# Moving the last two pa products of batch 1 ahead of the steps, and the activations' last subtractions of steps 1 to 11 to GpSimd

## The chip, the cores and the metric

The kernel runs on one core of a Trainium2 chip. The metric is the device time of one execution in microseconds, as the median of several runs; the core has five engines with queues of their own: TensorE (PE in the profile, with its weight loads as PEld), VectorE (DVE), ScalarE (ACT), GpSimd (POOL) and SyncE (SP), which here only issues transfers. ScalarE and GpSimd issue some transfers too. Each engine works through its own instructions in order and waits at an instruction until what it needs is there.

## The reference

A filter along the sequence by real Fourier transforms, and then an activation block on every token:

```
x: (8, 3008, 256)   filt_r, filt_i: (1505, 256)
w_in: (256, 2048)   w_out: (2048, 256)

X = rfft(x, axis=1)
Y = X * (filt_r + 1j * filt_i)
y = irfft(Y, n=3008, axis=1)

h = y.reshape(24064, 256) @ w_in
g = h / (1 + exp(-h))
out = g @ w_out
```

All is float32, and the weights arrive in a wider type (64-bit floats) that the kernel turns into float32 itself.

## The kernel before

**The activation block.** The tokens of a batch are taken in two halves of three pairs each, so there are 48 pairs (`token_pairs`), each of 2 x 256 tokens (240 in the last pair of a half). A pair takes eight steps, one for each pair of 128-wide slices of the 2048 hidden channels, so there are 384 steps. Both products are done as 2 x 2 blocks with seven products instead of eight. `hidden(step)` does the first seven (into the PSUM tiles `px` and `pyz`), with the sums between them: DVE forms g0, g2 and g1 from a product in PSUM and a copy in `abc` that ScalarE made, ScalarE applies silu to them, and DVE subtracts g[4:6] = g[1:3] - g[0:2]. `finish` makes the last two combinations, g6 = g2 - g4 and g7 = g3 - g6, and is called in the next step, right behind that step's g0. `project(step)` does the seven products of the second block into four accumulators `acc`; it runs one step later (`LAG = 1`), its products alternating with those of `hidden`. In it g6 and g7 are read by the last two products. `tokens(pair)` makes `ty`, the three combinations of y that the first products of a pair need.

**The order.** Nothing is scheduled automatically. Each step is cut into eight rounds. Every other piece of work (the Fourier stages of the next batches, the conversion of the weights, stores) is put at a step and a round by `put(step, rnd, piece)`; the list is sorted, and `until` emits the pieces whose time has come between the products of a step. So the place of a piece decides where it stands in each engine's queue. The first two pairs of batch 0 are taken in four parts (`PARTS`): steps 0 and 1 are of pair 0, steps 2 to 5 of pair 1, steps 6 to 11 of pair 0, and 12 to 15 of pair 1.

**The Fourier stages.** The sequence of 3008 is split as 94 rows by 32 columns. `pa` products (stage 1) transform the rows, `pb` products with the table `d_t` the columns, the filter is applied by DVE, `pc` products with `e_t` go back over the columns, and `pd` products (stage 3) with `wi_t` over the rows, giving y. Between the stages data go through DRAM (`d1`, `d2`) to change their layout. Batch 0 does all of this ahead of step 0, in room that later holds weights (`w_t`), with products that fill PE's pauses (`idle`); the other batches do it beside the steps of the batch before.

**Stage 1 of batch 1.** Eight units of x. Units 0 to 5 are three pairs p = 0, 1, 2, done ahead of step 0: `load_pair(p)` brings x in three 32-row slices for four column groups at once, `stage1_pair(p)` does 12 products on slices of 32 rows (line 432) into four PSUM banks, `out_pair` copies the banks out, and `store_rows` stores a unit with four transfers from GpSimd's queue. Units 6 and 7 are done in steps 7 and 8: `load_x` brings each to `x_all`, `stage1` does two products on 96 rows (line 452), ScalarE copies them out, and `store_rows` stores them. Their results are first read when batch 1's pb products begin, in step 11.

**PSUM banks ahead of step 0** are handed out in turn from eight (`bank`, counted by `early[0]`); a product waits until the bank's last content is copied out.

**The weights.** Sixteen tiles j, two for each pair of slices. A tile is loaded as raw words (`weights`), and converted in four parts on DVE with two activations on ScalarE between them: `bits` (lines 1222 and 1224), `converted` (ScalarE, lines 1231 and 1232), `added` (line 1238), `signed` (line 1243) and `placed` (line 1250), which writes w_t. When both tiles of a pair jp are placed, `combine_weights(jp)` makes the three combined blocks by four additions and subtractions. Tiles 0 to 3 are done ahead of step 0 and tiles 4 to 15 in steps 0 to 11, each before the step that reads it; the combining of jp 1 to 6 is done by GpSimd, of jp 0 and 7 by DVE.

**The order around the change**, ahead of step 0: the products of the pairs 0, 1 and 2, four idle products, then

```
    part["stage3"](0)
    part["stage3"](1)
    placed(2)
    part["stage3"](2)
    part["stage3"](3)
    placed(3)
    combine_weights(1, eng=gp)
    for u in range(4, 6):
        second["store_rows"](u)
    for g in (2, 3, 4, 5, 0, 1):
        for i in range(2):
            part["store_half"](g, i, 1, gp)
```

Here `stage3(g)` is 64 small pd products and the copying of their two banks to y, on ScalarE and DVE. `store_half(..., 1, ...)` stores the second half of the pc results, which stage 3 reads from step 11 on. `fetch_rows` (line 747) brings the first half back in the layout that the pd products of g = 0 to 3 read; the last fetch is issued by SP and ScalarE together.

Of the kernel before, what the change touches and what calls it, by code (L numbers as in the profile page):

```python
# [56 lines left out]
NS, NG = 24, 6  # L57
# [65 lines left out]
def second_pairs(x):  # L123

    rows = np.zeros((96, 32, C), x.dtype)
    rows[0:NR] = x.reshape(NR, 32, C)
    return rows.reshape(3, 32, 4, 4, 2 * C).transpose(2, 3, 1, 0, 4)[0:3].reshape(3, 128, 6 * C)
# [145 lines left out]
def kernel(  # L273
# [96 lines left out]
    def spectral(b):  # L370
# [54 lines left out]
        def stage1_pair(p):  # L425
# [406 lines left out]
        return dict(us=us, store_half=store_half, load_pair=load_pair, stage1_pair=stage1_pair, out_pair=out_pair, store_rows=store_rows, evict_y=evict_y, halves=halves, load_first=load_first, stage1_first=stage1_first, load_x=load_x, stage1=stage1, reverse_x=reverse_x,  # L832
# [15 lines left out]
    def plan(b, part):  # L848
# [153 lines left out]
    def tokens(pair):  # L1002

        n, yt = pairs[pair][3], channels(pair)
        t = typool.tile([128, 4, CH], FP32, name=f"ty_{pair}", tag="ty")
        combine(v, t[:, 0:2, 0:n], yt[:, :, n:2 * n],
                yt[:, 0, 0:2 * n].rearrange("p (a n) -> p a n", a=2), ALU.subtract)
        combine(v, t[:, 2, 0:n], yt[:, 1, n:2 * n], t[:, 0, 0:n], ALU.subtract)
        combine(v, t[:, 3, 0:n], yt[:, 1, 0:n], t[:, 2, 0:n], ALU.subtract)
        ty[pair] = t  # L1010

    def hidden(step):
# [24 lines left out]
        finish()  # L1037
# [295 lines left out]
    v.memset(blank, 0.0)  # L1333
    idle(12, operand=blank)
# [50 lines left out]
    part["forward"](5)  # L1385
    products(4)
# [57 lines left out]
    weights(4, 5)  # L1444
    second["load_x"](6)
    weights(6)
    second["load_x"](7)
# [9 lines left out]
    for step, rnd, *todo in (  # L1457
            (0, 5, (bits, 4)), (1, 0, (weights, 7, 8), (converted, 4)), (1, 1, (added, 4), (bits, 5), (signed, 4)),
            (1, 2, (weights, 9, 10)), (1, 5, (placed, 4), (added, 5)), (2, 0, (converted, 5)),
            (2, 1, (bits, 6), (signed, 5), (placed, 5)), (2, 3, (combine_weights, 2, None, gp)), (2, 5, (added, 6)),  # L1460
            (3, 0, (converted, 6)), (3, 1, (bits, 7), (signed, 6), (placed, 6)), (3, 3, (weights, 11)),
            (3, 5, (converted, 7), (added, 7)), (4, 1, (signed, 7), (placed, 7), (bits, 8)),
            (4, 3, (combine_weights, 3, None, gp), (weights, 12)), (4, 5, (converted, 8), (added, 8)),
            (5, 1, (signed, 8), (placed, 8), (bits, 9)), (5, 3, (weights, 13)), (5, 5, (converted, 9), (added, 9)),
            (6, 1, (signed, 9), (placed, 9), (bits, 10)), (6, 3, (combine_weights, 4, None, gp), (weights, 14)),
            (6, 5, (converted, 10)), (7, 1, (rounded, 10), (placed, 10)), (7, 2, (weights, 15)),
            (7, 3, (bits, 11), (added, 11)), (7, 5, (converted, 11), (bits, 12)), (8, 0, (converted, 12)),
            (8, 1, (signed, 11), (placed, 11), (added, 12)), (8, 2, (combine_weights, 5, None, gp)),
            (8, 3, (signed, 12), (placed, 12)), (8, 5, (bits, 13), (added, 13)), (9, 0, (converted, 13)),
            (9, 1, (bits, 14), (signed, 13), (placed, 13)), (9, 2, (combine_weights, 6, None, gp)),  # L1470
            (9, 5, (converted, 14), (added, 14), (bits, 15)), (10, 0, (converted, 15)),
            (10, 1, (signed, 14), (placed, 14), (added, 15)), (10, 5, (signed, 15), (placed, 15), (combine_weights, 7, 0)),
            (11, 1, (combine_weights, 7, 1))):
# [24 lines left out]
    for step in range(n_steps + LAG):  # L1498
# [3 lines left out]
        else:  # L1502
            finish()
# [51 lines left out]
```

## Time and profile before

| | us |
| --- | --- |
| median of 3 runs | 2499.95 (2499.06 to 2500.76) |
| the profiled execution | 2500.93 |
| its span, first to last instruction | 2499.1 |
| PE busy | 2479.1 |
| DVE busy | 1761.5 |
| ScalarE busy | 1092.3 |
| GpSimd busy | 458.4 |
| first pd product | 50.3 |
| first px product (start of step 0) | 56.7 |
| first px product of step 1 | 64.2 |
| first px product of step 11 | 135.8 |

The page gives each engine's busy time and, in 40 slices, how much of each slice it was busy. The chain that ended last is followed back from the last instruction, at each step to what released it. Groups of instructions are named by line, engine and operation, with what is written and read, and the idle time ahead of them with what ended it. The name in front of an arrow "<-" after an idle time is the engine and line that was waited for; "issue" is time in which the engine waited for nothing that the profile shows. Views of a stretch of time (timeline, busy times by stretch) use microseconds from the span's start. Outside the first 150 us and the last 100, PE is busy nearly without pause: 1600 us of the 1600 from 400 to 2000 us.

### The profile page before, as it was taken

To read this page: it belongs to the slowest core of one execution; us is meant where nothing else is said; L and a number is where in the kernel's file an instruction comes from. 1 tells how busy PE (TensorE), PEld (TensorE's weight loads), DVE (VectorE), ACT (ScalarE), POOL (GpSimd) and SP (SyncE) were. 2 spreads that over 40 slices of the span, in tenths; PEclk is the share of its full clock that TensorE was granted. 3 is DMA by queue.
4 is the path that set the end of the run, shared out by engine and by line. 5 is a ranking of instruction groups with operands and counts; after the bars stand their busy time and mean duration, and the time that the engine had idled before them with its cause. 6 is when DMAs were issued, how large, how long until landed. Compare 5 with 4: busy or idle time off the path is not lost.

```text
span 2499.1 us, 42322 instructions
## 1 busy us (share of the span) xinstructions
PE 2479.1 (99%) x16234; PEld 2125.2 (85%) x16234; DVE 1761.5 (70%) x3593; ACT 1092.3 (44%) x3001; POOL 458.4 (18%) x708
## 2 busy tenths in 40 slices
PE   9999999999999999999999999999999999999999
PEld 6778888888888888888888888889888888888988
DVE  7876677777777777777777867777677767655544
ACT  3634444444444444444444444444444444444443
POOL 4421112112121122211122112211221111101100
PEclk9999999999999999999999999999999999999999
DMA  8433233213242032420333203321142211200000
GB/s 303 147 88 103 67 72 82 72 37 81 60 96 72 23 93 53 114 63 20 82 75 100 55 26 91 79 68 43 35 107 54 56 43 35 63 21 9 17 9 17
DMA packets 139771, 170.68 MB, mean 68 GB/s; under 512 B 21053, under 2 KB 113565, under 8 KB 139037
## 3 DMA queue, kind: packets, MB, share of 16 engines
q1 hardware_dynamic: 115952, 121.15, 18.4%
q0 software_dynamic: 22656, 45.68, 7.0%
q8 instruction: 127, 2.08, 0.3%
q10 hardware_dynamic: 960, 1.16, 0.1%
q14 instruction: 76, 0.61, 0.1%
HBM read 96.06 MB, written 81.26 MB: 71 GB/s over the span
## 4 chain that ended last, share of the span: by engine, by line
PE 96%; DVE 2%; ACT 0%; issue 0%; POOL 0%; DMA 0%; DVEq 0%; POOLq 0%
PE acc L1093 45%; PE px L1025 25%; PE pyz L1025 19%; PE pd L800 1%; PE pf L522 1%; PE pc L618 1%; PE pb L580 1%; DVE g L996 1%; PE pc L696 0%; PE pa L402 0%; PE pb L562 0%; PE pd L762 0%; PE pa L432 0%; PE idle L1322 0%; DVE w_t L1250 0%
## 5 line engine op out<-in xcount | busy, mean ns | idle before, releaser
L1093 PE MATMUL acc<-g,w_t 128*128 128x256 f32 (+1 forms) x5376 | 1508.6, 376 | 3.2 <-ACT o L813 2.5
L1093 PEld LDWEIGHTS acc<-g,w_t 128*128 128x128 f32 x5376 | 1017.1, 190 | 153.5 <-ACT o L813 15.3
L996 DVE TENSOR_TENSOR g<-pyz,abc 128x256 f32<-128x256 f32 (+1 forms) x1152 | 479.6, 416 | 471.3 <-ACT abc L1046 231.4
L996 DVE TENSOR_TENSOR g<-g 128x256 f32<-128x256 f32 (+3 forms) x1152 | 591.2, 513 | 197.1 <-ACT g L1029 184.0
L1025 PE MATMUL px<-ty,w_t 128*128 128x256 f32 (+1 forms) x2304 | 677.5, 376 | 1.0 <-DVE ty L996 0.5
L1029 ACT ACTIVATE g<-g 128x256 f32<-128x256 f32 (+1 forms) x1152 | 472.8, 411 | 242.5 <-DVE g L996 242.5
L996 POOL TENSOR_TENSOR s<-s 128x256 f32<-128x256 f32 (+1 forms) x329 | 252.3, 784 | 1403.6 <-DVE s L1118 1044.8
L1025 PEld LDWEIGHTS px<-ty,w_t 128*128 128x128 f32 x2304 | 435.5, 190 | 55.9 <-issue 1.8
L1025 PE MATMUL pyz<-y,w_t 128*128 128x256 f32 (+1 forms) x1536 | 453.0, 377 | 6.6 <-DVE g L996 6.4
L1025 PEld LDWEIGHTS pyz<-y,w_t 128*128 128x128 f32 x1536 | 283.0, 190 | 52.9 <-DVE g L996 12.1
L1040 ACT COPY abc<-px 128x256 f32<-128x256 f32 (+1 forms) x384 | 141.3, 368 | 371.2 <-PE px L1025 371.2
L1046 ACT COPY abc<-px 128x256 f32<-128x256 f32 (+1 forms) x384 | 141.4, 368 | 311.6 <-PE px L1025 311.5
L1029 ACT ACTIVATE g<-px 128x256 f32<-128x256 f32 (+1 forms) x384 | 145.7, 380 | 299.3 <-PE px L1025 299.3
L1025 PE MATMUL px<-y,w_t 128*128 128x256 f32 (+1 forms) x768 | 227.8, 378 | 1.2 <-ACT g L1029 1.1
L1025 PE MATMUL pyz<-ty,w_t 128*128 128x256 f32 (+1 forms) x768 | 226.0, 376 | 0.0
L1025 PEld LDWEIGHTS px<-y,w_t 128*128 128x128 f32 x768 | 143.4, 189 | 24.9 <-ACT g L1029 3.9
L1025 PEld LDWEIGHTS pyz<-ty,w_t 128*128 128x128 f32 x768 | 142.5, 190 | 20.8 <-DVE g L996 0.6
L1033 ACT COPY abc<-px 128x256 f32<-128x256 f32 (+1 forms) x384 | 135.1, 352 | 35.2 <-PE px L1025 35.0
L542 POOL DMA_DIRECT2D d<-tf x96 | 48.7, 507 | 212.9 <-DVE tf L472 212.9
L1118 ACT COPY s<-acc 128x512 f32<-128x512 f32 (+1 forms) x94 | 54.2, 577 | 47.3 <-issue 28.5
L639 POOL DMA_DIRECT2D d<-low x36 | 22.1, 614 | 285.8 <-DVE low L635 275.1
L512 DVE TENSOR_TENSOR uf<-x_all 120x512 f32<-120x512 f32 (+1 forms) x72 | 60.2, 864 | 0.3 <-issue 0.3
(133 smaller groups left out, 1364.3 us busy)
## 6 DMA issues: line engine op xcount, KB each, us to landing
t<-d SPq DMA_DIRECT2D x84, 256.0 KB
t<-d SPq DMA_DIRECT2D x224, 96.0 KB
out_dram<-s SPq DMA_DIRECT2D x64, 256.0 KB
d<-q POOLq DMA_DIRECT2D x48, 256.0 KB, 5.2
x_all<-in_x_dram SPq DMA_DIRECT2D x96, 96.0 KB
x_all<-xr SPq DMA_DIRECT2D x96, 96.0 KB
d<-tf POOLq DMA_DIRECT2D x96, 96.0 KB, 2.7
d<-tq POOLq DMA_DIRECT2D x96, 96.0 KB, 2.8
```

The costliest lines, as they stand in the source:

```text
L512: nc.vector.tensor_tensor(out=out, in0=in0, in1=in1, op=op)
L522: nc.tensor.matmul(out=ps[q][32 * k:32 * k + 32], lhsT=wq_t[rows, k], rhs=rhs[k][rows], start=True, stop=True)
L542: nc.gpsimd.dma_start(out=d1[par, :, grp, at:at + 4], in_=part[rows].rearrange("p q n c -> p (q n) c"))
L580: nc.tensor.matmul(out=ps[k, ri][32 * j:32 * j + 32, a, :], lhsT=dn_t[rows, 4 * (g + a) + at, :], rhs=t2s[g + a][rows, at, :], start=True, ...
L996: eng.tensor_tensor(out=out, in0=in0, in1=in1, op=op)
L1025: nc.tensor.matmul(out=out, lhsT=w_t[:, jp, c, 0], rhs=rhs, start=start, stop=True, skip_group_check=True)
L1029: nc.scalar.activation(out=g[:, k, 0:n], in_=g[:, k, 0:n] if src is None else src, func=AFT.Silu)
L1033: nc.scalar.copy(out=sums[:, 0, 0:n], in_=xo)
L1040: nc.scalar.copy(out=sums[:, 1, 0:n], in_=xo)
L1046: nc.scalar.copy(out=sums[:, 2, 0:n], in_=xo)
L1093: nc.tensor.matmul(out=acc[pair][i][:, h, 0:n], lhsT=w_t[:, jp, OUT_PLACE.get(c, c), 1], rhs=g[:, k, 0:n], start=(new and h == 0), stop=la ...
L1118: copy(out=dst, in_=src)
```

## The change

The eight units of stage 1 of batch 1 are now four pairs, all ahead of step 0. The x of pair 3 is loaded into the room of the table `d_t` when batch 0's pb products have read it, and `d_t` is loaded again afterwards. The products of pair 3 stand between stage 3 of g = 1 and of g = 2. Pairs 2 and 3 are stored from SP by four transfers each (`store_pair`), of both units at once, and six of the twelve `store_half` transfers go from GpSimd's queue to SP's. Units 6 and 7 leave steps 7 and 8.

`finish` takes an engine: GpSimd in steps 1 to 11, DVE from step 12 on. `tokens` takes one too: pair 1 goes to GpSimd and is put at round 1 of step 0 instead of round 5 of step 1. The combining of jp = 7 goes to GpSimd. Ahead of step 0, both tiles 2 and 3 are placed, and combined by GpSimd, before the products of pair 3; the weights 4 to 6 are loaded earlier, and `bits` and `added` of tile 4 are done there. In the steps the conversions of two tiles are put together, and the places of all of them change.

```diff
-    return rows.reshape(3, 32, 4, 4, 2 * C).transpose(2, 3, 1, 0, 4)[0:3].reshape(3, 128, 6 * C)
+    return rows.reshape(3, 32, 4, 4, 2 * C).transpose(2, 3, 1, 0, 4).reshape(4, 128, 6 * C)
...
             if p == 0:
                 room = x_all.rearrange("p i a n -> p (i a n)")
+            elif p == 3:
+                room = d_t.rearrange("p s r n -> p (s r n)")
...
-            if p == 2:
-                t = s1pool.tile([128, 2, 2, 2, C], FP32, name=f"t1_{b}_{p}", tag="s1")
-                t = [t[:, i] for i in range(2)]
+            if p > 1:
+                pool, tag = (s1pool, "s1") if p == 2 else (gpool, "g")
+                us["t1", "pair", p] = pool.tile([128, 2, 2, 2, C], FP32, name=f"t1_{b}_{p}", tag=tag)
+                t = [us["t1", "pair", p][:, i] for i in range(2)]
...
+        def store_pair(p):
+            t1 = us.pop(("t1", "pair", p))
+            for k in range(4):
+                nc.sync.dma_start(out=d1[k // 2, :, k % 2, 8 * p:8 * p + 8],
+                                  in_=t1[32 * k:32 * k + NS].rearrange("p a h n c -> p (a h n) c"))
...
-        if b == 1:
-            for u in range(6, 8):
-                put(at + u - 47, 3, part["stage1"], u)
-        else:
+        if b > 1:
...
-    def tokens(pair):
+    def tokens(pair, eng=None):
+        eng = eng or v
...
-        combine(v, t[:, 2, 0:n], yt[:, 1, n:2 * n], t[:, 0, 0:n], ALU.subtract)
-        combine(v, t[:, 3, 0:n], yt[:, 1, 0:n], t[:, 2, 0:n], ALU.subtract)
+        combine(eng, t[:, 2, 0:n], yt[:, 1, n:2 * n], t[:, 0, 0:n], ALU.subtract)
+        combine(eng, t[:, 3, 0:n], yt[:, 1, 0:n], t[:, 2, 0:n], ALU.subtract)
...
-        finish()
+        finish(gp if step < 12 else v)
...
-    def finish():
+    def finish(eng):
         for g, n in unfinished:
-            combine(v, g[:, 6, 0:n], g[:, 2, 0:n], g[:, 4, 0:n], ALU.subtract)
-            combine(v, g[:, 7, 0:n], g[:, 3, 0:n], g[:, 6, 0:n], ALU.subtract)
+            combine(eng, g[:, 6, 0:n], g[:, 2, 0:n], g[:, 4, 0:n], ALU.subtract)
+            combine(eng, g[:, 7, 0:n], g[:, 3, 0:n], g[:, 6, 0:n], ALU.subtract)
...
+    gp.memset(x_all[:, 1, 1], 0.0)
...
     part["forward"](5)
+    second["load_pair"](3)
     products(4)
...
+    weights(4, 5)
+    second["store_pair"](2)
     idle(4)
+    early[0] += 7
     part["stage3"](0)
     part["stage3"](1)
-    placed(2)
+    placed(2, 3)
+    combine_weights(1, eng=gp)
+    bits(4)
+    second["stage1_pair"](3)
+    out_of(3, 0, 1, copy=act)
+    out_of(3, 2, copy=dve)
     part["stage3"](2)
+    out_of(3, 3, copy=act)
+    added(4)
     part["stage3"](3)
-    placed(3)
-    combine_weights(1, eng=gp)
-    for u in range(4, 6):
-        second["store_rows"](u)
-    for g in (2, 3, 4, 5, 0, 1):
+    second["store_pair"](3)
+    weights(6)
+    for g in (2, 3, 4):
         for i in range(2):
             part["store_half"](g, i, 1, gp)
     idle_wide(1)
     nc.sync.dma_start(out=wi_t, in_=wi_dram.ap())
-    weights(4, 5)
-    second["load_x"](6)
-    weights(6)
-    second["load_x"](7)
+    for g in (5, 0, 1):
+        for i in range(2):
+            part["store_half"](g, i, 1, nc.sync)
+    nc.sync.dma_start(out=d_t, in_=d_dram.ap())
...
-            (3, 0, (converted, 6)), (3, 1, (bits, 7), (signed, 6), (placed, 6)), (3, 3, (weights, 11)),
-            (3, 5, (converted, 7), (added, 7)), (4, 1, (signed, 7), (placed, 7), (bits, 8)),
...
+            (2, 1, (bits, 6), (added, 6), (bits, 7), (added, 7)), (2, 3, (combine_weights, 2, None, gp)),
+            (2, 5, (converted, 6)), (3, 0, (converted, 7)), (3, 1, (signed, 6), (placed, 6), (bits, 8), (signed, 7)),
+            (3, 3, (weights, 11)), (3, 5, (placed, 7)), (4, 0, (converted, 8), (weights, 12)),
...
-        step, rnd = combines[pair % per] if pair not in (1, 2) else ((1, 5), (12, 1))[pair - 1]
-        pending.append((pair // per * STEPS + step + rnd / ROUNDS, 98, lambda pair=pair: tokens(pair)))
+        step, rnd = combines[pair % per] if pair not in (1, 2) else ((0, 1), (12, 1))[pair - 1]
+        pending.append((pair // per * STEPS + step + rnd / ROUNDS, 98,
+                        lambda pair=pair: tokens(pair, gp if pair == 1 else None)))
```

More of the change, by code (lines that the diff above doesn't have):

```diff
@@ L830, in fold_wide @@
                 nc.vector.tensor_tensor(out=dst[:, :, :, at:at + n], in0=even[:, :, :, 0:n], in1=odd[:, :, :, 0:n], op=op)
-        return dict(us=us, store_half=store_half, load_pair=load_pair, stage1_pair=stage1_pair, out_pair=out_pair, store_rows=store_rows, evict_y=evict_y, halves=halves, load_first=load_first, stage1_first=stage1_first, load_x=load_x, stage1=stage1, reverse_x=reverse_x,
+        return dict(us=us, store_half=store_half, load_pair=load_pair, stage1_pair=stage1_pair, store_pair=store_pair, out_pair=out_pair, store_rows=store_rows, evict_y=evict_y, halves=halves, load_first=load_first, stage1_first=stage1_first, load_x=load_x, stage1=stage1, reverse_x=reverse_x,
                     load_fold=load_fold, fold=fold, stage1_fold=stage1_fold, evict_fold=evict_fold, pairs_fold=pairs_fold, forward_two=forward_two, free_two=free_two, multiply_two=multiply_two, add_two=add_two, inverse_two=inverse_two, even_two=even_two, rows_two=rows_two, ends_two=ends_two,
@@ L1000, in channels @@
         return y[b, half][:, :, c0:c0 + 2 * n]
-    def tokens(pair):
+    def tokens(pair, eng=None):
+        eng = eng or v
         n, yt = pairs[pair][3], channels(pair)
         t = typool.tile([128, 4, CH], FP32, name=f"ty_{pair}", tag="ty")
-        combine(v, t[:, 0:2, 0:n], yt[:, :, n:2 * n],
+        combine(eng, t[:, 0:2, 0:n], yt[:, :, n:2 * n],
                 yt[:, 0, 0:2 * n].rearrange("p (a n) -> p a n", a=2), ALU.subtract)
-        combine(v, t[:, 2, 0:n], yt[:, 1, n:2 * n], t[:, 0, 0:n], ALU.subtract)
-        combine(v, t[:, 3, 0:n], yt[:, 1, 0:n], t[:, 2, 0:n], ALU.subtract)
+        combine(eng, t[:, 2, 0:n], yt[:, 1, n:2 * n], t[:, 0, 0:n], ALU.subtract)
+        combine(eng, t[:, 3, 0:n], yt[:, 1, 0:n], t[:, 2, 0:n], ALU.subtract)
         ty[pair] = t
@@ L1457 @@
     for step, rnd, *todo in (
-            (0, 5, (bits, 4)), (1, 0, (weights, 7, 8), (converted, 4)), (1, 1, (added, 4), (bits, 5), (signed, 4)),
-            (1, 2, (weights, 9, 10)), (1, 5, (placed, 4), (added, 5)), (2, 0, (converted, 5)),
-            (2, 1, (bits, 6), (signed, 5), (placed, 5)), (2, 3, (combine_weights, 2, None, gp)), (2, 5, (added, 6)),
-            (3, 0, (converted, 6)), (3, 1, (bits, 7), (signed, 6), (placed, 6)), (3, 3, (weights, 11)),
-            (3, 5, (converted, 7), (added, 7)), (4, 1, (signed, 7), (placed, 7), (bits, 8)),
@@ L1463 @@
[L1463 to L1472, printed above, removed]
@@ L1473 @@
-            (11, 1, (combine_weights, 7, 1))):
+            (0, 5, (converted, 4), (bits, 5)), (1, 0, (weights, 7, 8), (converted, 5)),
+            (1, 1, (added, 5), (signed, 4), (placed, 4), (signed, 5)), (1, 2, (weights, 9, 10)), (1, 5, (placed, 5)),
+            (2, 1, (bits, 6), (added, 6), (bits, 7), (added, 7)), (2, 3, (combine_weights, 2, None, gp)),
+            (2, 5, (converted, 6)), (3, 0, (converted, 7)), (3, 1, (signed, 6), (placed, 6), (bits, 8), (signed, 7)),
+            (3, 3, (weights, 11)), (3, 5, (placed, 7)), (4, 0, (converted, 8), (weights, 12)),
@@ new lines @@
+            (4, 1, (added, 8), (bits, 9), (signed, 8), (placed, 8)), (4, 3, (combine_weights, 3, None, gp)),
+            (4, 5, (converted, 9), (added, 9), (weights, 13)),
+            (5, 1, (signed, 9), (placed, 9), (bits, 10), (added, 10)),
+            (5, 3, (combine_weights, 4, None, gp), (weights, 14)), (5, 5, (converted, 10), (bits, 11)),
+            (6, 0, (converted, 11)), (6, 1, (signed, 10), (placed, 10), (added, 11), (signed, 11)), (6, 3, (weights, 15)),
+            (7, 1, (placed, 11), (bits, 12), (added, 12), (bits, 13)), (7, 3, (combine_weights, 5, None, gp)),
@@ L1474 @@
+            (7, 5, (converted, 12), (added, 13)), (8, 0, (converted, 13)),
+            (8, 1, (signed, 12), (placed, 12), (signed, 13), (placed, 13)), (8, 3, (combine_weights, 6, None, gp)),
+            (8, 5, (bits, 14)), (9, 0, (converted, 14)), (9, 1, (added, 14), (bits, 15), (signed, 14), (placed, 14)),
+            (9, 5, (converted, 15), (added, 15)), (10, 1, (signed, 15), (placed, 15)),
+            (10, 2, (combine_weights, 7, None, gp))):
         for piece, *args in todo:
@@ L1502 @@
         else:
-            finish()
+            finish(v)
         if step >= LAG:
```

## The prediction

> **What bounds the kernel now.** I read the page first: busy times and the chain of waits.
>
> ```profile
> PE 2479.1 (99%) x16234; PEld 2125.2 (85%) x16234; DVE 1761.5 (70%) x3593; ACT 1092.3 (44%) x3001; POOL 458.4 (18%) x708
> PE 96%; DVE 2%; ACT 0%; issue 0%; POOL 0%; DMA 0%; DVEq 0%; POOLq 0%
> ```
>
> TensorE (PE) is busy 99% and the chain is PE for 96%. So a change can win only by taking matmuls off PE, or by closing the 20 us in which PE is idle. Next I cut the first steps at the start of each step's first px matmul (from PE's timeline) and asked for busy times by stretch (columns: stretch, length, PE, PEld, DVE, ACT, POOL, clock, DMA):
>
> ```profile
> 70.34:77.73 7.39, 6.32 (x30) 5.22 (x28) 6.80 (x16) 4.58 (x12) 5.02 (x10) 1.00 0.93 286
> 84.34:90.77 6.43, 6.39 (x30) 5.18 (x29) 5.70 (x11) 3.78 (x10) 1.97 (x3) 1.00 0.34 129
> 104.70:112.73 8.03, 8.03 (x32) 5.99 (x32) 6.24 (x13) 4.72 (x12) 1.72 (x4) 1.00 0.25 79
> 128.09:135.76 7.67, 6.41 (x30) 5.34 (x30) 7.08 (x14) 3.88 (x10) 2.58 (x3) 1.00 0.84 163
> 167.78:173.82 6.04, 6.04 (x29) 5.32 (x28) 4.50 (x10) 2.42 (x8) 0.00 (x0) 1.00 0.13 54
> ```
>
> A step with nothing late takes 6.04 us (14 matmuls); steps 2, 4, 7 and 10 take 7.39, 6.43, 8.03 and 7.67. The ten steps from 64.20 (step 1) to 135.76 (step 11) take 71.56, that is 60.4 of full pace, 3.44 of pa products and **7.7 us lost**. Step 11 takes 11.53 where its 16 matmuls, two pd and one pb need 6.91 + 2.22 + 1.02 = 10.15: **1.4 lost**. In all 9.1. PE's waits from 56 to 150 us say on whom:
>
> ```profile
> PE pyz L1025 <- DVE g L996: 4.2, 5, 1.3
> PE px L1025 <- ACT g L1029: 1.1, 2, 0.8
> ```
>
> VectorE (DVE), which in these steps also converts the weights, is late with the g that frees pyz. The last thing to see is what DVE suffers while GpSimd (POOL) combines weights:
>
> ```profile
> 117.08 4.20 POOL L996 TENSOR_TENSOR w_t<-w_t 128x256 f32<-128x256 f32 x4 [3.84 <-PE acc L1093]
> ...
> 117.47 1.22 DVE L1243 SCALAR_TENSOR_TENSOR e<-raw,e 128x512 uint32<-128x512 uint32 x1
> 118.72 1.10 DVE L1250 SCALAR_TENSOR_TENSOR w_t<-m,e 128x512 f32<-128x512 f32 x1
> 119.74 0.41 DVE L996 TENSOR_TENSOR g<-pyz,abc 128x256 f32<-128x256 f32 x1
> ```
>
> The same two forms take 0.69 elsewhere; the operation that reads PSUM keeps its 0.41. Summed over the groups of 60 to 150 us, mean of each form against its undisturbed 0.418 or 0.683: L1224 12 x 0.179, L1222 12 x 0.062, L1238 10 x 0.071, L1243 10 x 0.056, L1250 10 x 0.050, g<-g 0.2: 4.9 us for 20 combining operations, **0.243 us of DVE per POOL operation**, and 0.53 in the worst row.
>
> **Part 1: pa products.** Units 6 and 7 leave steps 7 and 8. Each is two 96x512 products, shown as four records and 1.72 us in the chain, with nothing beside it on PE: **-3.44**. ScalarE loses four 0.59 copies there and POOL eight store issues, neither of them on the path.
>
> ```profile
> 54.24 1.33 issue
> ...
> 108.42 1.72 PE pa L452 x4
> ```
>
> They return as pair 3 between pd 1 and pd 2: 12 products on 32-row slices. L432 took 5.60 for two such pairs, so +2.80. Against it, the 1.33 hole in the pd products. It is no wait for data. By the chain's counts 57 + 72 + 8 + 244 = 381 matmuls lie between it and the other such hole (36.43), close to 3 x 128, and 127 packets of the instruction queue for 2 x 16234 PE instructions are 256 each: code that arrived late while pd ran at 16 ns a product. With 2.8 us of slow products put in after the previous block's start, the next block has time: -1.33. pd then ends at 56.0 + 1.5 = 57.5. On DVE the addition of tile 4 (0.60, up to 0.53 more beside POOL) now stands before the last eviction of y, which ends at about 58.5, and ty 0 starts there instead of 57.11: +1.4. But placing tile 3 no longer stands in front, and POOL, whose store issues end at 56.1, has done its combining by 59.2 instead of 60.8, so ty's last two operations should cost 0.89 instead of 1.75. I take **+1.0** for the start (0 to 2.5).
>
> **Part 2: transfers.** SP gains the x of pair 3 (768 KB, ahead of the stores of q 2), eight stores of 192 KB, six q stores that leave POOL, and d's reload (768 KB); it loses two loads of 384 KB. The reload is first read by the pb of step 11 near 146 us, some 80 us later. Weights 4 and 5 now load right behind the fetch of rows for pd. That fetch has little slack: in the DMA view of 49 to 50 us
>
> ```profile
> q10 hardware_dynamic: 44, 0.04, 12.2%
> ```
>
> is still its last piece (issued by ScalarE at 44.7), and pd starts at 50.31. 768 KB at the 336 to 354 GB/s of 31 to 33 us are 2.3 us, but from 38 to 39 only 0.03 MB move, so part falls into a hole and part under the idle products: **+0.5** (0 to 2.3).
>
> **Part 3: DVE and POOL.** POOL takes ty 1 (about 1.5 + 2 x 0.78) and 22 of the activations' subtractions, two in each of steps 1 to 11; DVE loses 0.79 a step, 1.5 for ty 1 and 1.6 of the last combining. In POOL's queue: combining to 59.2, six store issues of 0.58 to 62.8 (each waits for the issue eight before it, the last of which start by 56.1 and land 2.8 later), ty 1 to 66. Its reader is step 2 near 71. The first pair of subtractions ends near 68, its reader (the S2 product of step 1) comes 4.4 us after that step's start, near 69.6: covered by 1.5, and charged nothing; what is late after that is PE itself. In later steps g[4:6] is ready 1.8 us after the start and two operations at 0.91 (POOL's mean there) end at 3.8, also ahead of 4.4 and 5.2. Combining comes behind them.
>
> DVE's new need: per step g1, the wait for its silu, g4:5, g0, g2 = 0.90 + 0.61 + 0.34 + 0.34 = 2.19 by the distances of starts. A tile's conversion is 0.67 + 0.60 + 0.72 + 0.60 = 2.6; twelve are 31.2, of which the new order has 1.3 ahead of step 0, 0.7 in it and 1.3 in step 10, so 27.9 in steps 1 to 9, with 1.9 of drains. Steps 1 to 9: 19.7 + 27.9 + 1.9 = 49.5, against 9 x 6.04 = 54.4 of PE. POOL does 38 operations beside them (18 subtractions, 20 combinings): 38 x 0.243 = 9.2. 58.7 - 54.4 = 4.3 lost. The same sum for before falls 1.5 short of what was lost in steps 1 to 9, since one overfull step can't borrow from the next; there single steps hold up to 4.7 of conversions and ty, now 3.6 at most, so I add 0.4, and 0.2 for steps 10 and 11. 4.9 lost instead of 9.1: **-4.2**. Ends: at no contention 0.6 lost (-8.5); at 0.53 a piece 15.2 + 0.6 = 15.8 lost (+6.7).
>
> The Trainium skill, SBUF — State Buffer, "Who interferes with whom", says that a DVE instruction with two SBUF inputs, or in a two-port mode, and a GpSimd one that reads SBUF lock each other out for the whole instruction. The PSUM reader's 0.41 and the 1.22 above agree; the mean of 0.243 is far milder.
>
> **Sum:** -3.44 + 1.0 + 0.5 - 4.2 = -6.1. The profiled run took 2500.93 (span 2499.1 and 1.83 around it), 0.98 above the median, so it becomes 2494.8, and the median of 2499.95 becomes **2493.9**.
>
> **Rivals.**
> Contention at its worst row. Every POOL operation holds DVE for 0.53: 15.8 lost, -3.44 + 1.5 + 6.7 = +4.8, or 2504.7, and more if POOL's own results come late. It decides from 0.40 us a piece on, where 38 x 0.40 - 4.9 + 0.6 = 10.9 are lost, 1.8 more than before, and the 3.44 - 1.5 of the rest is used up. For it: the subtractions start right where DVE's conversions start, with two SBUF inputs each. Against: only the 117 and 127 us combinings come near it. The rule of the Trainium skill named above, taken strictly, gives this case. Chance 0.15.
>
> No contention, since POOL yields (its combining took 3.09 to 4.20 for the same four operations): -3.44 + 1.0 - 8.5 = -10.9, 2489.0. Chance 0.13.
>
> The loop, not DVE's load, costs the steps: silu 3 stands behind 1.44 of conversions on ScalarE, and DVE waits 6.2 us for silu in all. Then the subtractions do not do what they are moved for, the converted tiles only change places, and what is left is -3.44 + 1.5 = -1.9: 2498.0. For it: step 4 lost 0.39 with a light load. Against: the longest waits stand behind ty and conversions. Chance 0.15.
>
> Transfers: rows for pd come 2.3 late and the code hole stays: -3.44 - 4.2 + 1.0 + 2.3 + 1.3 = -3.0, 2496.9. Chance 0.15.
>
> **Numbers.** Forecast 0.42, its own range 2490.5 to 2497.5. About 5 us (0.2%) either way can't be told from no change. Of the forecast's 0.42 some 0.34 lies beyond -5, with the no-contention case 0.13 and 0.05 of the transfers: faster 0.52. Slower: the worst contention, 0.15, where it is joined by a late start. The rest, 0.33, is no change. The range of 2488 to 2504 leaves out some 0.1 above and 0.07 below.
>
> **What would show it.** pa at L452 gone from steps 7 and 8 and the px after it 1.72 earlier; pd with pa inside and no issue hole; pd 0 still starting near 50.4; ty 0 ready near 60.5; steps 1 to 9 of 6.1 to 6.9 us; L1222 to L1250 slower by some 9 us in sum over the same stretch. Wrong if PE waits for POOL's g, if steps 2 to 9 stay above 7, or if pd 0 starts after 52.

## The result, and the profile after

The changed kernel takes 2512.2 us (median of 6 runs, 2507.29 to 2515.8), the kernel before 2500.24 in the runs beside it (2499.06 to 2500.76): a ratio of 1.0046, with a 95% interval of 1.0033 to 1.0059. It is 12 us slower where 6 us faster was forecast. The profiled execution took 2508.4 (span 2506.4), 3.8 below its own median, so a part of the loss has to be looked for in what differs from one execution to the next.

The profile page of the changed kernel, busy times and the chain's shares:

```profile
PE 2478.8 (99%) x16250; PEld 2123.0 (85%) x16250; DVE 1764.6 (70%) x3565; ACT 1094.1 (44%) x3000; POOL 471.9 (19%) x716
...
PE 95%; DVE 3%; ACT 1%; issue 0%; DMA 0%; POOL 0%; SPq 0%; ACTq 0%; DVEq 0%
```

PE is as busy as before in a span that is 7.3 us longer. DVE is no less busy (1764.6 after 1761.5) though 22 subtractions, a ty and a combining have left it, and POOL's busy time rises by 13.5 only. All of the loss lies in the first 155 us. Starts of a step's first px product, before and after:

| step | before | after | later by |
| --- | --- | --- | --- |
| 0 | 56.74 | 63.47 | 6.7 |
| 1 | 64.20 | 69.60 | 5.4 |
| 11 | 135.76 | 144.15 | 8.4 |
| 12 | 147.29 | 154.58 | 7.3 |

So in these two executions 5.4 us come from ahead of step 1, 3.0 from steps 1 to 10, and step 11 gives 1.1 back. (Between them step 0 gives 1.3 back; the kernel before ran it at half clock here, from 57.18 to 64.01.) PE's timeline of the start (start, length, work, count, and in brackets the idle time before it and what ended it), first of the kernel before, then of the changed one:

```profile
50.31 3.92 PE L762 MATMUL pd<-wi_t,w_t 64*64 64x47 f32 x244
55.56 0.44 PE L762 MATMUL pd<-wi_t,w_t 64*64 64x47 f32 x12 [1.33 <-issue]
```

```profile
50.11 1.16 PE L1329 MATMUL idle<-wx_t 96*128 96x128 f32 x8
51.32 0.32 PE L771 MATMUL pd<-wi_t,w_t 64*64 64x47 f32 x2
52.78 1.97 PE L771 MATMUL pd<-wi_t,w_t 64*64 64x47 f32 x114 [1.15 <-ACT e L1239]
55.88 0.44 PE L771 MATMUL pd<-wi_t,w_t 64*64 64x47 f32 x12 [1.13 <-issue]
56.25 2.86 PE L434 MATMUL pa<-d_t,wx 32*128 32x512 f32 x24
59.04 1.64 PE L771 MATMUL pd<-wi_t,w_t 64*64 64x47 f32 x92
61.90 0.80 PE L771 MATMUL pd<-wi_t,w_t 64*64 64x47 f32 x36 [1.22 <-issue]
```

The first pd product starts 1.0 later than before, then stops for 1.15 (the line names ScalarE, but the part of the last fetch of rows that ScalarE issues had packets on their way until 52.1 here, and until 49.5 before), and the hole with no releaser is there twice, not gone. The steps by stretch (length, then busy time of PE, PEld, DVE, ACT, POOL, the clock, DMA share and GB/s), and PE's waits from 63 to 150 us:

```profile
75.75:84.44 8.69, 6.31 (x29) 5.23 (x28) 7.94 (x12) 4.87 (x12) 5.18 (x6) 1.00 0.73 279
84.44:92.17 7.73, 7.73 (x29) 6.46 (x28) 5.72 (x12) 3.74 (x9) 1.46 (x2) 0.78 0.31 80
92.17:100.33 8.16, 6.32 (x30) 5.24 (x29) 7.44 (x10) 5.03 (x12) 5.71 (x6) 1.00 0.28 72
114.95:123.76 8.81, 6.31 (x30) 5.19 (x28) 8.29 (x13) 3.77 (x9) 5.46 (x6) 1.00 0.01 2
138.11:144.15 6.04, 6.04 (x29) 5.32 (x28) 4.06 (x7) 2.40 (x7) 3.32 (x5) 1.00 0.00 0
```

```profile
PE pyz L1032 <- DVE g L1002: 9.8, 9, 2.5
```

Steps 2, 4 and 7 hold a whole conversion beside 5 us of POOL's work and are DVE's: 7.4 to 8.3 busy. PE waits 9.8 us for DVE where it waited 4.2. Step 3 is another matter: PE is busy all of its 7.73 us with 6.04 us of work, at a granted clock of 0.78.

### The profile page after: what moved, and what is told of

Same layout as the page of the kernel before. It is cut to its first block, busy times and chain, and to the rows that moved or that the text cites. A ratio compares the mean times of both kernels' runs of the same rounds, so it can differ in the third digit from the quotient of the medians.

```text
span 2506.4 us, 42323 instructions
## 1 busy us (share of the span) xinstructions
PE 2478.8 (99%) x16250; PEld 2123.0 (85%) x16250; DVE 1764.6 (70%) x3565; ACT 1094.1 (44%) x3000; POOL 471.9 (19%) x716
## 4 chain that ended last, share of the span: by engine, by line
PE 95%; DVE 3%; ACT 1%; issue 0%; DMA 0%; POOL 0%; SPq 0%; ACTq 0%; DVEq 0%
PE acc L1100 45%; PE px L1032 25%; PE pyz L1032 19%; PE pd L809 1%; PE pf L531 1%; PE pc L627 1%; PE pb L589 1%; DVE g L1002 1%; PE pa L402 0%; PE pd L771 0%; DVE m L1231 0%; PE pb L571 0%; DVE w_t L664 0%; DVE e L1229 0%; DVE m L1245 0%
## 5 line engine op out<-in xcount | busy, mean ns | idle before, releaser
L1002 DVE TENSOR_TENSOR g<-g 128x256 f32<-128x256 f32 (+2 forms) x1130 | 582.6, 516 | 196.4 <-ACT g L1036 183.7
```

The lines of the kernel that those rows point to most:

```text
L1002: eng.tensor_tensor(out=out, in0=in0, in1=in1, op=op)
```

## The experiments

Each ran beside the kernel before on the same chip. "Clock" is span times one less the granted clock, as a mean over the runs: what a slower clock took away at most. (The granted clock is on record to three places, so a single run's figure is good to 1.25 us either way.)

| kernel | us | before | ratio (95%) | clock |
| --- | --- | --- | --- | --- |
| the change | 2512.2 | 2500.24 | 1.0046 (1.0033 to 1.0059) | 5.4 |
| sub_on_dve | 2511.75 | 2499.95 | 1.0043 (1.0031 to 1.0056) | 5.0 |
| sub_only | 2511.2 | 2499.95 | 1.0048 (1.0035 to 1.006) | 7.5 |
| sub_twice | 2519.16 | 2499.95 | 1.0076 (1.0061 to 1.0092) | 5.0 |
| fetch_on_sp | 2509.53 | 2499.95 | 1.0038 (1.0026 to 1.0051) | 4.5 |
| pa_only | 2506.6 | 2501.27 | 1.0023 (1.0014 to 1.0033) | 1.8 |
| x3_behind_rows | 2508.3 | 2501.27 | 1.0033 (1.002 to 1.0046) | 5.0 |
| pair3_first | 2507.72 | 2501.27 | 1.0026 (1.0015 to 1.0036) | 4.3 |
| third_of_pair3 | 2508.34 | 2501.58 | 1.0027 (1.0018 to 1.0037) | 6.5 |
| half_pa_left_out | 2500.26 | 2501.58 | 0.9992 (0.9983 to 1.0001) | 0.5 |
| ten_long_pauses | 2570.06 | 2501.27 | 1.0274 (1.026 to 1.0288) | 27.6 |
| ten_short_pauses | 2529.46 | 2501.58 | 1.01 (1.0083 to 1.0117) | 8.8 |
| after_again | 2511.47 | 2501.05 | 1.004 (1.0028 to 1.0053) | 6.5 |
| filled_pauses | 2516.97 | 2501.05 | 1.006 (1.0047 to 1.0074) | 4.5 |
| best_of_change | 2510.31 | 2501.05 | 1.0036 (1.0022 to 1.005) | 1.3 |
| filled_pauses_2 | 2509.33 | 2501.8 | 1.0029 (1.0018 to 1.004) | 2.2 |
| best_of_change_2 | 2505.2 | 2501.8 | 1.001 (1.0001 to 1.002) | 2.0 |

The runs of the kernel before lost 0.2 to 2.8 to the clock, and that differs on one chip too (0.2 beside `pa_only`, 1.6 beside `filled_pauses_2`).

### GpSimd's subtractions

`sub_on_dve` is the changed kernel with the subtractions back on DVE:

```diff
-        finish(gp if step < 12 else v)
+        finish(v)
```

> The changed kernel with the last subtractions (g6, g7) of steps 1 to 11 back on VectorE; all else stays. Theory LOCK: each GpSimd operation keeps VectorE's conversions waiting, 16.8 us in sum over 42 operations of steps 1 to 11 in the changed kernel, 0.40 each. Then the 22 subtractions cost VectorE as much on GpSimd (22 x 0.40 = 8.8) as on VectorE itself (22 x 0.395 = 8.7), and undoing them leaves the steps about as long: step 1 to step 11 within 2 us of 74.6, the time within 3 us of the changed kernel's at the same granted clock, and the conversions' means down by some 8 us in sum. Rival RELIEF: GpSimd really takes work off VectorE, and without it the steps grow by 6 to 9 us. Rival START: all the loss lies ahead of step 0, and the steps change by less than 1 us.

It takes as long as the change, within the intervals: the 6 to 9 us of RELIEF are not there. Why, the groups of DVE's work from 69 to 144 us tell (busy us, mean ns, idle). First the changed kernel, with the subtractions on POOL:

```profile
L1245 DVE SCALAR_TENSOR_TENSOR m<-raw,m 128x512 f32<-128x512 uint32 x10 | 9.7, 966 | 0.1
L1257 DVE SCALAR_TENSOR_TENSOR w_t<-m,e 128x512 f32<-128x512 f32 x10 | 9.4, 942 | 0.3
L1250 DVE SCALAR_TENSOR_TENSOR e<-raw,e 128x512 uint32<-128x512 uint32 x10 | 9.4, 938 | 0.0
L1231 DVE TENSOR_SCALAR m<-raw 128x512 uint32<-128x512 uint32 x11 | 8.8, 804 | 0.0
L1229 DVE TENSOR_SCALAR e<-raw 128x512 uint32<-128x512 uint32 x10 | 7.9, 785 | 0.0
```

Then `sub_on_dve`:

```profile
L1002 DVE TENSOR_TENSOR g<-g 128x256 f32<-128x256 f32 x22 | 10.5, 476 | 0.4
...
L1245 DVE SCALAR_TENSOR_TENSOR m<-raw,m 128x512 f32<-128x512 uint32 x10 | 7.7, 768 | 0.1
L1257 DVE SCALAR_TENSOR_TENSOR w_t<-m,e 128x512 f32<-128x512 f32 x10 | 6.9, 690 | 0.3
L1250 DVE SCALAR_TENSOR_TENSOR e<-raw,e 128x512 uint32<-128x512 uint32 x10 | 6.9, 687 | 0.0
L1231 DVE TENSOR_SCALAR m<-raw 128x512 uint32<-128x512 uint32 x10 | 6.9, 687 | 0.0
L1229 DVE TENSOR_SCALAR e<-raw 128x512 uint32<-128x512 uint32 x10 | 5.4, 539 | 0.0
```

The 22 subtractions cost DVE 10.5 us when it does them. When POOL does them, these five conversion groups take 45.2 instead of 33.8 (one more L1231 among them, 0.7): 10.7 us more. POOL did 20 subtractions in this stretch, since the pair of step 11 falls behind it, so that is 0.53 for each, against the 0.48 that it saved. (Ten g[4:6] subtractions are 0.6 cheaper in all, 724 ns for 782, which makes it 0.50.) DVE is relieved of nothing: its other work takes as much longer as the subtractions would have taken. Steps 1 to 10 took 71.40 in `sub_on_dve` and 74.55 in the change, 1.7 of it the slow clock of step 3; that is outside the 2 us that LOCK allowed. But this execution of `sub_on_dve` is the fastest of its five, 6.7 under their median, with no half-rate stretch before the end.

`sub_only` is the kernel before with the subtractions on POOL in steps 1 to 11, and nothing else:

```diff
-        finish()
+        finish(gp if step < 12 else v)
...
```

> The kernel before with nothing but the subtractions of steps 1 to 11 moved to GpSimd; pa, conversions and transfers as before. LOCK: no gain; step 1 to step 11 stays at 70 to 74 us (71.56 before), the conversions' sum grows by 5 to 9 us, time within 2 us of before's. RELIEF: the step's stalls go, 64 to 67 us, time 5 to 7 us shorter. START: same as RELIEF or no change, since nothing ahead of step 0 moves.

Its time, 11.25 us over the kernel before, was forecast wrong by all theories, for a reason in POOL's queue (first PE's wait, then POOL's timeline):

```profile
PE acc L1093 <- POOL g L996: 8.0, 1, 8.0
```

```profile
62.63 3.14 POOL L996 TENSOR_TENSOR w_t<-w_t 128x256 f32<-128x256 f32 x4 [5.45 <-DVE w_t L1250]
65.72 4.16 POOL L465 DMA_DIRECT2D d<-t  x8
72.93 3.31 POOL L720 DMA_DIRECT2D d<-q  x6 [3.06 <-DMA d<-t]
...
79.52 1.54 POOL L996 TENSOR_TENSOR g<-g 128x256 f32<-128x256 f32 x2
```

The first subtractions stood behind twenty store issues; the change has fourteen of these stores on SP. Behind that wait the ten steps 2 to 11 took 77.02, the first 1.4 us of them at half clock; in the kernel before they took 76.95. Taken alone, the move to POOL is worth less than 1 us there.

`sub_twice` is the changed kernel with the steps' subtractions done twice on POOL.

> The changed kernel with every subtraction of steps 1 to 11 done twice on GpSimd (the same values again), so 22 operations more on GpSimd and none on VectorE. LOCK: VectorE's conversions lose another 22 x 0.3 to 0.5, and the time grows by 5 to 11 us, with the waits of PE for VectorE's g. RELIEF: VectorE does not feel it; the time grows by less than 2 us, unless PE waits for GpSimd's g itself, which the view of waits would name.

It lost 7 us more than the change, inside LOCK's 5 to 11. PE waited 4.3 us for POOL's g besides 8.8 for DVE's, so both the lock and POOL's own lateness are in it, and it doesn't tell them apart.

### The pa products and the start

`pa_only` is the kernel before with pair 3 ahead of the steps, and no other part of the change:

```diff
+    second["load_pair"](3)
...
+    second["stage1_pair"](3)
...
+    second["store_pair"](3)
...
-    second["load_x"](6)
-    second["load_x"](7)
+    nc.sync.dma_start(out=d_t, in_=d_dram.ap())
```

> The kernel before with nothing but the pa part: pair 3 between pd 1 and pd 2, its x loaded where the changed kernel loads it, stored by SP, d_t loaded again; conversions, subtractions, combining and the other transfers as before. If the loss ahead of step 0 belongs to the pa part (2.8 us of products, late rows, code holes), the first px product comes 4 to 7 us later than 56.7, step 0 gives 1 to 1.5 of it back, and steps 7 and 8 give back 1 to 3 (their pa was 3.44, but VectorE is nearly full there): 2500 to 2504. If the pa part was sound as I predicted (-3.44 + 1.0 + 0.5), 2496 to 2499, and all of the loss is the rest's.

It is 5.3 us slower than before, which its expectation had as 0 to 4 if the loss lay in the pa part. In its profiled execution the first px product came at 62.71, 6.0 later, and step 1 took 10.09 us for 6.14, with a wait of 1.99 for DVE's g and a half-rate stretch behind it. Step 7 took 7.50 without its 1.72 of pa, where before it took 8.03 with it; step 8 took 8.11 against 8.08. So 0.50 of 3.44 us came back: in the place of the products PE waits for DVE's g, 1.09 us in step 7 and 1.83 in step 8, where it had no such wait before. `half_pa_left_out` asks for the same with nothing added at the start (ScalarE's copies and the stores stay):

```diff
-            for h in range(2):
+            for h in range(1 if b == 1 and u > 5 else 2):
                 nc.tensor.matmul(
...
```

> The kernel before, with the second of the two products of units 6 and 7 of the second batch left out in steps 7 and 8 (both copies then read the first product, so part of the second batch's first transform is not computed). That is 1.72 us of TensorE of the prediction's 3.44, and nothing is added at the start. GIVEN BACK (the prediction's view, TensorE bound in steps 7 and 8): the two steps fall from 8.03 and 8.08 to 7.2 each, and the time by 1.7 to about 2498.2. COVER (VectorE and its waits set these steps, as pa_only's steps of 7.50 and 8.11 without those products say): the two steps fall by no more than 0.5 us in sum and the time stays within 0.5 us of the kernel before.

Step 8 of the kernel before, and then the two steps of `half_pa_left_out` by stretch, columns as above:

```profile
112.73:120.81 8.08, 8.08 (x33) 6.10 (x33) 7.42 (x13) 5.01 (x12) 4.16 (x6) 1.00 0.27 70
...
104.46:112.12 7.66, 7.44 (x30) 5.53 (x31) 6.23 (x14) 4.63 (x12) 1.72 (x5) 1.00 0.28 82
112.12:120.19 8.07, 7.51 (x30) 5.64 (x31) 7.37 (x13) 5.11 (x12) 3.98 (x5) 1.00 0.25 69
```

Of 1.72 us of products left out, 0.37 came off step 7 and 0.01 off step 8. PE, which had no pause in these steps before, now has 0.22 and 0.56: the products had filled time that DVE needed anyway. The time itself fell by 1.3 us, with an interval from 4.3 faster to 0.3 slower, so it can't tell 0.4 from 1.7; the steps can.

At the start three kernels varied the changed one. `fetch_on_sp` issues both halves of the last fetch of rows from SP; `x3_behind_rows` puts `load_pair(3)` behind that fetch; `pair3_first` puts pair 3's products in the place of the four idle ones ahead of pd:

```diff
-    idle(4)
-    early[0] += 7
+    second["stage1_pair"](3)
...
     part["stage3"](0)
```

> The changed kernel with the second half of the last fetch of rows issued by SP in front of the loads of weights 4 and 5, not by ScalarE beside them. Theory TRANSFER: that half (256 KB in 1 KB pieces on ScalarE's queue) shares the transfer engines with the 1 MB of weights behind it and lands at 52.3 instead of 49.4, which holds pd's second product until 52.78. Then pd runs on without the 1.15 us hole, and the first px product comes 0.8 to 1.4 us earlier than 63.47. Rival: the hole is a wait for ScalarE's conversion, as the view of waits names it; then nothing moves.

> The changed kernel with the load of pair 3's x (768 KB) moved from in front of the stores of q 2 to behind the last fetch of rows. With the last fetch on SP the second pd product still came 2.1 us late, so it is not only ScalarE's queue. Theory X3: the 768 KB stand in SP's queue ahead of the q stores and the fetches, and push the rows back by up to 2.3 us. Then the pd products run on from where the idle products end (the hole of 1.15 us behind the first two goes), and the first px product comes 1 to 2 us earlier, at 61.5 to 62.5 with the same start. Rival WEIGHTS: the 1 MB of weights 4 and 5 behind the fetch delays it; then the hole stays, and pair 3 may wait for its own x as well.

> The changed kernel with the products of pair 3 ahead of all pd products, in place of the four idle ones, so that PE works while the rows come. The hole behind the first two pd products should go, and pair 3's 2.8 us be half hidden: the first px product 2 to 3.5 us earlier than in the changed kernel (60 to 61.5), unless the code holes grow, since 256 pd products then run without a slow one between them.

First px products came at 64.37, 65.03 and 61.75 (63.47 in the change). One execution of each decides little, as the start differs from one execution to the next. Five profiled executions start as the kernel before does (its own, `sub_only`, `half_pa_left_out` and the two with ten pauses, which change later steps only), six as the change does (its own, `after_again`, `sub_on_dve`, `sub_twice`, `filled_pauses` and `filled_pauses_2`). Means in us; the three columns in the middle add up time between the first pd product and the first px:

| | first pd | pa | holes without a releaser | other pauses | first px (lowest to highest) | step 1 |
| --- | --- | --- | --- | --- | --- | --- |
| five like before | 50.95 | 0 | 2.49 | 0 | 58.88 (56.28 to 61.86) | 65.45 |
| six like the change | 51.43 | 3.66 | 3.36 | 1.25 | 65.39 (62.72 to 67.86) | 72.67 |

So the change's start costs 6.5 us up to the first px and 7.2 up to step 1. The products are the largest part of it (2.86 at full clock, more where a half-rate stretch fell on them); the holes grew by 0.9 and did not close.

The first px of `fetch_on_sp` and `x3_behind_rows` lie within the change's own range, so neither transfer shows an effect by itself; in `x3_behind_rows` a hole of 3.56 us stood behind the first two pd products. `pair3_first`, at 61.75, lies below that range and still has one hole of 2.96. `third_of_pair3` is `pair3_first` with two of the three slices of pair 3 left out, 8 of the 12 products.

> pair3_first with 32 of pair 3's 48 products left out (only the first of the three slices of its sum; the second batch's units 6 and 7 are not computed in full). Their time at the start falls from 2.80 to about 0.93 us, by 1.87; pair3_first took 2507.7 with its first px at 61.75. PRODUCTS (the products themselves push everything behind them): first px at 59.9, 2505.9. ARRIVAL (what pd needs, its rows or its instructions, arrives late whatever stands ahead of it): the pause ahead of or inside pd grows by about what is left out, first px at 61.2 to 61.8, and 2507 to 2508.

Some 1.87 us of products less, and the time is about the same (1.0027 and 1.0026 of before; the intervals are wider than 1.87 us, so they don't exclude a gain). In its profiled execution pd even began late, with pauses of 1.80, 1.91 and 1.32, and the first px came at 65.09, beyond what both theories had; its last rows were on their way until 55.6. This fits ARRIVAL, but one execution doesn't prove it. The holes that no row explains end with a packet: the records of the instruction queue have one of 16384 bytes ahead of each.

| kernel | packet, from and to | PE goes on | hole |
| --- | --- | --- | --- |
| before | 53.02 to 54.24 | 55.56 | 1.33 |
| half_pa_left_out | 51.00 to 51.96 | 53.36 | 1.48 |
| half_pa_left_out | 54.50 to 55.48 | 56.81 | 1.32 |
| the change | 53.32 to 54.32 | 55.88 | 1.13 |
| the change | 59.50 to 60.47 | 61.90 | 1.22 |
| third_of_pair3 | 57.63 to 58.64 | 59.98 | 1.91 |
| after_again | 55.27 to 56.23 | 57.59 | 3.78 |
| filled_pauses | 56.70 to 57.67 | 59.24 | 4.62 |

PE goes on 1.31 to 1.58 us behind the packet's end in every row. The 18 profiled executions have 26 such holes in pd, of 0.27 to 4.62 us, and each ends 1.23 to 1.87 us behind a packet. From one hole to the next there are 128 products (a weight load and a matmul each) where pd runs without other work. PE's timeline of `after_again`, the changed kernel itself:

```profile
51.85 1.97 PE L771 MATMUL pd<-wi_t,w_t 64*64 64x47 f32 x114 [0.52 <-ACT e L1238]
57.59 0.66 PE L771 MATMUL pd<-wi_t,w_t 64*64 64x47 f32 x12 [3.78 <-issue]
58.19 4.16 PE L434 MATMUL pa<-d_t,wx 32*128 32x512 f32 x24
```

pd eats a block in 2 us, and the next was 3.8 us away. In the change the DMA engines were busy for 1.01 and 0.89 of 48 to 52 and 52 to 56 us, before for 0.84 and 0.53. That the blocks came late because of this load fits in part: but they come late in the kernel before too, by 2.49 us in the mean of the table, and no run took the load away.

### The clock

A half-rate stretch is one in which the granted clock is 0.50. The trace records when the granted clock changes. In all profiled runs the half-rate stretches last 3.41 us or a multiple of it (but for the last, which the end cuts), and start on a grid of 3.41 us that runs through the execution. Two pauses of the changed kernel, cut at that grid (PE busy, clock, DMA share, GB/s):

```profile
81.21:84.63 3.42, 1.04 (x5) 1.00 0.26 107
84.63:88.04 3.41, 3.41 (x9) 0.50 0.02 5
118.76:122.17 3.41, 1.96 (x10) 1.00 0.02 5
122.17:125.58 3.41, 2.36 (x11) 1.00 0.00 0
```

The pause of 2.38 us at 81.5 lay in one stretch of the grid, PE was busy for 0.30 of it, and in the next the clock was 0.50. The pause of 2.50 at 120.7 was shared by two stretches, and nothing followed. From step 1 to the last 10 us, over all 18 profiled runs, each full-rate stretch of the grid with under 0.45 busy was followed by a half-rate one, none with 0.46 or more was, and those of 0.45 went both ways. (In the last 10 us, where the work runs out, stretches of 0.46, 0.47 and 0.48 were followed by one too.) So where a pause falls decides, and that differs between executions. It fits the spread of the change from 2507 to 2516: the six spans less what the clock took lie between 2502.7 and 2505.0.

Two kernels made ten pauses in the long even part of the kernel before, by doing the subtraction g[4:6] several times in ten steps:

```diff
+        for _ in range(7 if step in range(64, 384, 32) else 1):
```

> The kernel before with the subtraction of g[4:6] done seven times over in ten steps spread over the run (64, 96 and on), the same values each time: 6 x 0.61 us of VectorE more in each, so that PE pauses once for some 3 us at full pace. Theory CLOCK: after such a pause the granted clock halves for about 3.4 us, as seen behind the 2.4 and 8 us pauses of the changed kernel and of the one with the subtractions alone; each pause then costs its own 3 and up to 1.7 more: +40 to +48 us, clock 0.990 to 0.994. Rival: the clock does not follow such pauses; +28 to +32, clock as before (0.998 to 1.0).

> The kernel before, with VectorE's subtraction g[4:6] done four times (not seven, as in ten_long_pauses) in the same ten steps, so that TensorE pauses about half as long. ten_long_pauses cost 70 us, of which span times clock gave 42 as pauses (4.2 each) and 28 as reduced clock (2.8 each). DOSE (the clock falls in proportion to the pause): half of both, 2533 to 2537, mean clock .994 or .995. THRESHOLD (only pauses above some 2.4 us halve the clock): the pauses of about 2 us cost their own length alone, 2515 to 2523, clock .998 or more, and no row of 0.85 us for a product behind a short pause.

With seven subtractions all ten pauses had a half-rate stretch behind them, of 3.41 or 6.83 us, and the clock took 27.6 us, 2.8 a pause; with four, three of ten had one, and it took 8.8. The sign is the clock theory's, though the first kernel lost 68.8 us where 40 to 48 were forecast: the pauses themselves took some 41, not 30. Neither DOSE (2533 to 2537) nor THRESHOLD (2515 to 2523) has the second number: a short pause costs the clock either nothing or one or two whole stretches.

`filled_pauses` was to keep the changed kernel's waits and fill them with spare products; in it and in `best_of_change` the first block's sums of those four steps are changed.

```diff
+        for _ in range({2: 4, 4: 3, 5: 2, 7: 4}.get(step, 0)):
+            mm(zo, A12, yt[:, 1, 0:n], True)
         mm(yo, S4, yt[:, 1, n:2 * n], False)
```

> The changed kernel, with 4, 3, 2 and 4 spare products (0.43 us each, the step's A12 product done again into its own place, whose sum VectorE has read long before) ahead of the last S4 product of steps 2, 4, 5 and 7, where TensorE waited 2.38, 1.84, 1.31 and 2.50 us for VectorE. The waits stay; TensorE is busy in them. CLOCK (the halved stretches behind these pauses cost what the mean clock of .9978 says, 5.4 us over six runs): no half-rate stretch in steps 1 to 10, mean clock .9990 or more, 3 to 4 us under after_again, about 2508 to 2509. WORK (the clock's fall hits TensorE where it waits anyway, and costs next to nothing): within 1 us of after_again, or above it where a filler stands in the way.

> The changed kernel unchanged, for its time on this chip: 2510 to 2514, mean clock .997 to .999. In its profiled run the half-rate stretches, if the grid rule holds, start where a stretch of 3.41 us before them has TensorE busy under about half: behind the waits of steps 2, 4 or 7, not in every one of them.

> pair3_first with the last subtractions on VectorE and 2, 2, 2 and 4 spare products in steps 2, 4, 5 and 7. pair3_first alone took 6.5 us more than the kernel before, of which 4.1 were clock. CLOCK and LOCK together: about 2503 to 2505, still 2 to 5 above the kernel before, because the start stage's 3 to 4 us are not given back by steps 7 and 8. Were the prediction's 3.44 us of TensorE real, it would come to 2498 or less.

It missed its aim, as PE's timeline shows:

```profile
88.78 2.43 PE L1032 MATMUL pyz<-y,w_t 128*128 128x256 f32 x10 [2.39 <-DVE g L1002]
```

The spare products wrote the tile that DVE still read, so they waited with the rest and then took their own time: 5.5 us over `after_again`, where 3 to 4 less were expected. `best_of_change`, with the same spare products, came out at 2510.31 for 2503 to 2505. The time of `after_again` came where it was expected. Its half-rate stretches did not: they lie at 57 and 68 us of its profiled run, with none behind the pauses of steps 2, 4 and 7, whose stretches of the grid were 0.48, 0.49 and 0.64 busy. The second attempt gives the spare products a bank of their own:

```diff
+        if step in {2: 9, 4: 7, 5: 5, 7: 9}:
+            idle({2: 9, 4: 7, 5: 5, 7: 9}[step])
         mm(yo, S4, yt[:, 1, n:2 * n], False)
```

> filled_pauses put its spare products behind the waits, not into them, and each took its full time. Here the spare products go to a bank of their own that nothing reads: 9, 7, 5 and 9 products of 96x128 on 128 columns (about 0.22 us each, so 2.0, 1.5, 1.1 and 2.0 us) ahead of the last S4 product of steps 2, 4, 5 and 7 of the changed kernel, whose waits of 2.38, 1.84, 1.31 and 2.50 us for VectorE should shrink by as much in the record while the steps keep their lengths (8.69, 8.16, 7.62 and 8.81). CLOCK: no half-rate stretch in steps 2 to 8, span times clock as in the changed kernel (2503 to 2504), the clock's loss 2 to 3 instead of 5 to 6, so 2508 to 2509. WORK: 2511 to 2513.

> best_of_change with its spare products in a bank of their own (5, 5, 5 and 9 of them in steps 2, 4, 5 and 7). best_of_change lost 1.3 to the clock but had 10 spare products of 0.43 us behind its waits, 4.3 us; without that 2506 (2510.3 less 4.3), still 4 to 6 above the kernel before, by the start stage. Were the prediction's 3.44 us of TensorE real, 2503 or less.

Timeline and step 2 of `filled_pauses_2`:

```profile
85.35 2.17 PE L1331 MATMUL idle<-wx_t 96*128 96x128 f32 x18
87.90 0.70 PE L1032 MATMUL pyz<-y,w_t 128*128 128x256 f32 x2 [0.39 <-DVE g L1002]
```

```profile
79.73:88.44 8.71, 8.32 (x48) 7.40 (x46) 7.97 (x13) 4.84 (x11) 5.19 (x6) 1.00 0.33 131
```

The step keeps its length (8.69 in the change), the wait shrinks to 0.39, and no half-rate stretch is left from step 1 on. The clock takes 2.2 us instead of 5.4 and 6.5, and the time is 7.5 over before instead of 10.4 and 12.0. That is the 3 us that were expected, though the intervals of the ratios still overlap. `best_of_change_2` (pair 3 first, subtractions on DVE, pauses filled) is the fastest form of the change that was run, 3.4 over before, and within 1 us of its expected 2506. None beats the kernel before.

## Why the prediction was wrong, by its own steps

The profiled span grew by 7.3 us where 6.1 less were forecast, 13.4 apart: 3.9 of that lie ahead of step 1, and 9.5 in steps 1 to 11.

- **-3.44 for the pa products (part 1).** "With nothing beside it on PE" was right, and the wrong question. The removed products are worth what their step is not waiting for already: 0.38 of 1.72 in `half_pa_left_out`, 0.50 of 3.44 in `pa_only`. The prediction had step 7 at 8.03 with PE busy throughout, and read full PE as PE-bound. DVE's g came at nearly the same time without the products: in `pa_only` PE waited 2.92 us for it in the two steps.
- **+1.0 and +0.5 for the start (parts 1 and 2).** Measured at step 1: +5.4 in the profiled executions, +7.2 by the means of five and six. The products were sized right (2.86 at full clock against 2.80), but the hole was charged as filled (-1.33) where two came; in the means the holes grew by 0.9. The reading that the holes are late code was right, as the packets show; that slow products give the next block time was wrong. The last rows came 2.7 us later, as the fourth rival had it, with no gain shown from moving a transfer alone.
- **-4.2 for DVE and POOL (part 3).** The term fails at its price: 0.243 us of DVE for each POOL operation, averaged over combinings that mostly ran where DVE had little to do. From 69 to 144 us of the change it is 0.40 (16.8 us over 42 operations, same undisturbed lengths), exactly the break-even that the prediction named, and 0.50 to 0.53 for the subtractions by themselves. At 0.40 its own sum had 10.9 us lost in steps 1 to 11; 14.4 were, or 12.7 without the slow clock. The rival of contention had the right mechanism, at the price of its worst row; its 2504.7 still counted the 3.44 as a gain. The Trainium skill, SBUF — State Buffer, "Who interferes with whom", has the two engines lock each other out where both need the ports that they share. This trace agrees: 10.1 to 10.7 us of DVE's time were paid for 9.5 saved.
- **Not in the sum: the clock.** The profiled execution of the kernel before has a half-rate stretch of 6.83 us, in step 0, and the prediction left the clock out. Mean spans differ by 11.5 us (2509.4 and 2497.9, the change's six runs and the nine runs of before beside `sub_on_dve`); of these 4.6 are clock (5.4 and 0.8). The other 6.9 are pauses and work. The Trainium skill, TensorE: Matmul & The Clock Gate, "Part 1: The HAM clock gate (the "warmup" mystery)", has the free-running window of 3413 ns, and this trace agrees. Its section "HAM oscillation — how this bites in real kernels" warns of pauses above some 3.4 us; here 2.38 us were enough.
- **What held.** The first subtractions did not keep PE waiting, because the change took POOL's stores away; PE waited for POOL's g only in `sub_only` and `sub_twice`. pa did leave steps 7 and 8. Of the signs of being wrong, one came for the most part: steps 2 to 5, 7 and 9 took more than 7 us. A second nearly did: the first pd product started at 51.32, ahead of the 52 that was named, but the rest of pd only at 52.78.

Left open: what delays the instruction blocks, in the kernel before too, and why the start differs by some 5 us from one execution to the next.

## What to carry to other kernels

Before counting a product that leaves a step, ask when the step's slowest other engine would let it end: an engine that is full because it fills another's time gives nothing back. Work on 32-bit SBUF operands that goes from DVE to GpSimd beside DVE's own was free of charge only on paper here: 0.50 to 0.53 us were paid for 0.48 saved. Count pauses of PE twice, for their length and for the half-rate stretch that may follow, and give a pause that can't be closed spare products in a bank that nobody reads.

## What was not expected of the hardware

- The half-rate clock follows a grid of 3.41 us: in the steps, less than about 0.45 of a grid stretch busy halves the next, and a pause of 2.4 us can do so or not, by where it falls. In the start stage, with its many small products, a stretch of 0.61 was followed by half rate and one of 0.48 was not.
- Small products can outrun their own code: 128 pd products and their weight loads take 2 us and are one packet of 16384 bytes; 26 holes of 0.3 to 4.6 us ended 1.23 to 1.87 us after a packet. The Trainium skill, Runtime: NRT & Kernel Launch, "Instruction fetch mechanics", has blocks of that size and calls their cost mostly hidden; here it was in the open.
